# Weight conversion emitted as three interleaved stages, with a reordered start, in a linear-attention and bilinear feed-forward kernel

## The chip, the cores and the metric

The kernel runs on one core of one Trainium2 chip. The metric is the device time of one execution in microseconds (us). The engines named below are TensorE (PE for its matmuls, PEld for its weight loads), VectorE (DVE), ScalarE (ACT), GpSimd (POOL) and SyncE (SP, which here only issues DMAs). Each engine runs its own instructions strictly in the order in which they were emitted; between engines only semaphores order the work. Line numbers (L179) are those of the kernel before.

## The reference

Gated linear attention over 4 batches, 8 heads, 768 positions and 48 channels, then a bilinear feed-forward network on the 3072 tokens:

```python
f = 1.0 / (1.0 + np.exp(-f_logit))
for t in range(S):
    state = f[:, :, t, :, None] * state + np.einsum('bhd,bhe->bhde', k[:, :, t], v[:, :, t])
    y[:, :, t] = np.einsum('bhd,bhde->bhe', q[:, :, t], state)
x = y.transpose(0, 2, 1, 3).reshape(B * S, H * D)      # 3072 x 384
out = ((x @ w_a) * (x @ w_b)) @ w_out                  # 384 -> 1536 -> 384
```

The attention inputs are float32. The three weight matrices come as float64, which no engine computes with.

## The kernel before

**Units.** Attention is cut into 16 units: a batch, a half of the sequence (384 positions) and four of the eight heads. Four sets of input tiles (q, k, f, v) are used in rotation; `load_unit(u)` (L119) issues seven DMAs on SP, and `across(u)` (L315) calls it for unit u+4 when it is done with a set. `front(u)` (L190) makes the decays on ACT, POOL and DVE: two sigmoids (L195, L196), two POOL operations (L198, L199), an ACT operation (L200), then DVE scans (L204, L210) and products into q and k (L206, L211). It is a generator, cut by `yield` into parts that the main program calls one at a time. `scores` (L227), `turn` (L251: transposes of k through the PSUM tile ps_x, and a copy kT), `gains` (L261: matmuls into ps_x, then sums st on DVE), `within` (L298) and `across` (matmuls into ps_y, copies y, DMAs of y into xT issued from ACT's queue, L351) follow. From unit 2 on, `slot(u)` (L400) strings these parts together in six calls.

**Feed-forward.** The tokens form eight blocks of 384. `ffn(blk)` (L356) is a generator: twelve steps of six matmuls each (L366) with a copy b_sb on ACT (L374) and a product ab on DVE (L376), then the matmuls with w_out (L386). In block 0 these last come in twelve groups of three, one group for each 128 rows of w_out, elsewhere in three groups of twelve. The PSUM pool ps_f has four banks for all of this.

**Weights.** `pieces()` (L134) cuts the three matrices into 36 pieces of 128 x 384: w_b and w_a in turn for each of the twelve columns of 128, then the twelve rows of w_out. `load_weights()` (L145) issues the DMA of the next piece, as 64-bit words, into a buffer of a rotating pool "raw" of three. `from_double` (L163) turns a piece into float32 with eight operations on three engines, L173 to L182: ACT takes the absolute value and the sign of the high words, POOL clamps, DVE shifts and masks and scales the low words, POOL adds, ACT takes the absolute value, DVE applies the sign. `convert(n)` (L154) converts pieces one after the other until n are done, and calls `load_weights()` behind each.

**Order.** All of the main program stands under `tc.manual_schedule()` (L432), so each engine keeps the order of emission. The program from L455 to L483 starts units 0 to 2 by hand with convert(1), (2), (4) and (6) in between. The loop from L491 runs the blocks; ahead of each feed-forward step it calls the slot parts that are due by a table of due steps (L488) and, in block 0, `convert`, so that two pieces are emitted for each of the steps i=1 to 9, two more at i=10, and then one for each i. Piece 35, the last, is emitted at i=20.

A buffer of a rotating pool is given to a new tile when the last reader of the old tile has run, whatever the order in which the two were emitted; the instruction that writes the new tile waits for it in its own engine's queue.

Of the kernel before, what the change touches and what calls it, by code (L numbers as in the profile page):

```python
# [10 lines left out]
FP32 = mybir.dt.float32  # L11
I32 = mybir.dt.int32
U32 = mybir.dt.uint32
# [3 lines left out]
C = 128  # L17
FINE = (0, 1, 2, 4, 8, 16)
BLK = 384
PIECE = 384  # L20
# [3 lines left out]
K_EXP = 75.0  # L24
# [12 lines left out]
@with_exitstack  # L37
def kernel(
    ctx: ExitStack,
    tc: tile.TileContext,  # L40
    q: bass.AP,
    k: bass.AP,
    f_logit: bass.AP,
    v: bass.AP,
    masks: bass.AP,
    moe_w_a: bass.AP,
    moe_w_b: bass.AP,
    moe_w_out: bass.AP,
    out: bass.AP,
):  # L50
    nc = tc.nc
    DFF, DM = moe_w_out.shape[0], out.shape[1]
    NKT, NFT = DM // 128, DFF // 128

    const = ctx.enter_context(tc.tile_pool(name="const", bufs=1))

    def fixed(shape, name, dtype=FP32):
        return const.tile(shape, dtype, tag=name, name=name)

    ident = fixed([128, 128], "ident")  # L60
    w_a = fixed([128, NKT, DFF], "w_a")
    w_b = fixed([128, NKT, DFF], "w_b")
    w_out = fixed([128, NFT, DM], "w_out")
    bad = fixed([1, 1], "bad", I32)
    weights = (w_a, w_b, w_out)

    make_identity(nc, ident)
    with ExitStack() as pools:
        by_quotients(pools, tc, q, k, f_logit, v, moe_w_a, moe_w_b, moe_w_out, out, ident, weights, bad)
    again = nc.values_load(bad[0:1, 0:1], min_val=0, max_val=1, skip_runtime_bounds_check_because="it is a comparison's result")  # L70
    with tc.If(again > 0), ExitStack() as pools:
        by_levels(pools, tc, q, k, f_logit, v, masks, out, ident, weights)


def by_quotients(ctx, tc, q, k, f_logit, v, moe_w_a, moe_w_b, moe_w_out, out, ident, weights, bad):
    nc = tc.nc
# [4 lines left out]
    NQ = H // 4  # L81
    NC = BLK // C
# [8 lines left out]
    sb2 = ctx.enter_context(tc.tile_pool(name="sb2", bufs=2))  # L91
    sb4 = ctx.enter_context(tc.tile_pool(name="sb4", bufs=4))
    ab_pool = ctx.enter_context(tc.tile_pool(name="ab", bufs=NFT + 1))
    raw_pool = ctx.enter_context(tc.tile_pool(name="raw", bufs=3))
    ps_a = ctx.enter_context(tc.tile_pool(name="ps_a", bufs=1, space=bass.MemoryType.PSUM))
    ps_f = ctx.enter_context(tc.tile_pool(name="ps_f", bufs=4, space=bass.MemoryType.PSUM))

# [11 lines left out]
    zeros = fixed([128, BLK], "zeros")  # L109
# [6 lines left out]
        b, r = divmod(u, NH * NQ)  # L116
        return (b, *divmod(r, NQ))

    def load_unit(u):  # L119
        if u >= NU:  # L120
            return
        b, half, qd = unit(u)
        t = sets[u % NSET]
        cols = slice(half * BLK, half * BLK + BLK)
        for nm, src in (("f", f_logit), ("k", k), ("q", q)):
            heads = src[b].rearrange("(n two) d s -> two d n s", two=2)
            for par in range(2):
                nc.sync.dma_start(out=t[nm][R * par:R * par + D], in_=heads[par][:, 2 * qd:2 * qd + 2, cols])
        nc.sync.dma_start(
            out=t["v"].rearrange("s n c x -> s n (c x)"),  # L130
            in_=v[b, 2 * qd:2 * qd + 2, :, half * NC:half * NC + NC].rearrange("n s c two d -> s n (c two d)"),
        )

    def pieces():  # L134

# [9 lines left out]
    def load_weights():  # L145
        if len(raws) < len(todo):
            dst, src, shape = todo[len(raws)]
            raw = dst
            if src.dtype != FP32:
                raw = raw_pool.tile([128, *shape], mybir.dt.uint64, tag="raw", name="raw")  # L150
            nc.sync.dma_start(out=raw, in_=src)
            raws.append(raw)

    def convert(n):  # L154

        while done[0] < min(n, len(todo)):
            dst, src, shape = todo[done[0]]
            if src.dtype != FP32:
                from_double(dst, raws[done[0]], shape)
            done[0] += 1  # L160
            load_weights()

    def from_double(dst, raw, shape):  # L163

        words = raw.bitcast(U32).rearrange("p k (n two) -> p (k n) two", two=2)
        lo, hi = words[:, :, 0], words[:, :, 1]  # L170
        h, r, sign = (sb2.tile([128, PIECE], FP32, tag=n, name=n) for n in ("h", "r", "sign"))
        hu, ru = h.bitcast(U32), r.bitcast(U32)
        nc.scalar.activation(h, hi.bitcast(FP32), AF.Abs)  # L173
        nc.scalar.activation(sign, hi.bitcast(FP32), AF.Sign)
        nc.gpsimd.tensor_scalar(h, h, HI_MAX, HI_MIN, ALU.min, ALU.max)  # L175
        nc.vector.tensor_scalar(hu, hu, 3, 0x40000000, ALU.logical_shift_left, ALU.bitwise_xor)  # L176
        nc.vector.tensor_scalar(ru, hu, 0xFF800000, None, ALU.bitwise_and)  # L177
        nc.vector.scalar_tensor_tensor(out=r, in0=lo, scalar=2.0**-52, in1=r, op0=ALU.mult, op1=ALU.mult)  # L178
        nc.gpsimd.tensor_tensor(h, h, r, ALU.add)  # L179
        nc.scalar.activation(h, h, AF.Abs)  # L180
        h, sign = (x.rearrange("p (k n) -> p k n", k=shape[0]) for x in (h, sign))
        nc.vector.tensor_tensor(dst, h, sign, ALU.mult)  # L182

    live = {}
    xT = {}
# [4 lines left out]
    def front(u):  # L190

        t = sets[u % NSET]
        x = halves(t["f"])
        f, inv, fix = (sb2.tile([128, 2 * BLK], FP32, tag=n, name=n) for n in ("f", "inv", "fix"))
        nc.scalar.activation(f, x, AF.Sigmoid)  # L195
        nc.scalar.activation(inv, x, AF.Sigmoid, bias=less, scale=-1.0)  # L196

        nc.gpsimd.tensor_scalar(inv, inv, math.exp(K_EXP), 1.0, ALU.mult, ALU.add)  # L198
        nc.gpsimd.tensor_tensor(fix, f, inv, ALU.mult)  # L199
        nc.scalar.activation(fix, fix, AF.Identity, bias=two, scale=-1.0)  # L200
        yield
        for n in range(2):
            c = slice(n * BLK, n * BLK + BLK)
            nc.vector.tensor_tensor_scan(x[:, c], f[:, c], zeros, math.exp(MIDDLE), ALU.mult, ALU.add)  # L204
        nc.vector.tensor_scalar(held[:, u], t["f"][:, :, BLK - 1], math.exp(MIDDLE - DECAY_MAX), None, ALU.is_ge)
        nc.vector.tensor_tensor(halves(t["q"]), halves(t["q"]), x, ALU.mult)  # L206
        yield
        for n in range(2):
            c = slice(n * BLK, n * BLK + BLK)
            nc.vector.tensor_tensor_scan(inv[:, c], inv[:, c], fix[:, c], math.exp(-MIDDLE), ALU.mult, ALU.mult)  # L210
        nc.vector.tensor_tensor(halves(t["k"]), halves(t["k"]), inv, ALU.mult)  # L211
        live[u] = {}
        yield
# [34 lines left out]
        )  # L248
        live[u]["at"] = at

    def turn(u):  # L251
        kf = halves(sets[u % NSET]["k"])
        kT = sb1.tile([128, 2, NC, 128], FP32, tag="kT", name="kT")
        for n in range(2):
            for c in range(NC):
                o = n * BLK + c * C
                nc.tensor.transpose(ps_x[:, n, c * C:c * C + C], kf[:, o:o + C], ident)  # L257
        nc.scalar.copy(kT.rearrange("s n c x -> s n (c x)"), ps_x[:, :, 0:BLK])
        live[u]["kT"] = kT

    def gains(u):  # L261
# [169 lines left out]

    with tc.manual_schedule():  # L432
        nc.scalar.preload_act_table_set("sigmoid_and_others")
        for i in range(NSET):
            for n, eng, x in (("f", nc.gpsimd, 30.0), ("k", nc.gpsimd, 0.0), ("q", nc.vector, 0.0)):
                eng.memset(sets[i][n], x)
            if i < NQ:
                load_unit(i)
        for ps in (ps_x, ps_y):
            nc.vector.memset(ps, 0.0)  # L440
        for x, value in ((zeros, 0.0), (less, -K_EXP), (two, 2.0)):
            nc.gpsimd.memset(x, value)
        nc.gpsimd.memset(causal, 1.0)
        for p in range(2):
            half = causal[SUB * p:SUB * p + SUB]
# [2 lines left out]
            )  # L448
        nc.gpsimd.memset(ones, 1.0)
        done = [0]  # L450
        for _ in range(3):
            load_weights()


        fronts = [front(u) for u in range(NQ + 1)]  # L455
        for u in range(NQ):
            next(fronts[u])
            next(fronts[u])
        convert(1)
        for u in range(NQ):  # L460
            next(fronts[u])
        for u in range(NQ, NSET):
            load_unit(u)
        scores(0)
        turn(0)
        convert(2)
        gains(0)
        next(fronts[2])
        within(0)
        scores(1)  # L470
        turn(1)
        across(0)
        next(fronts[2])
        convert(4)
        gains(1)
        next(fronts[2])
        within(1)
        slots = {s: slot(s) for s in range(NQ, NU + 1)}
        next(slots[NQ])
        next(slots[NQ])  # L480
        next(slots[NQ])
        across(1)
        convert(6)  # L483
# [1 line left out]

        queue = []
        for s in slots:
            for d in (0, 1, 2.2, 3.4, 4.6, 5.8)[3 if s == NQ else 0:]:  # L488
                queue.append(((s - NQ) * (NFT + NTG) / 2 - 6 + d, s))
        queue.sort(reverse=True)  # L490
        for blk in range(NBLK):  # L491
# [369 lines left out]
```

## Time and profile before

| | |
|---|---|
| median of 3 runs | 789.6 us (789.41 to 790.02) |
| profiled execution: its time | 789.36 us |
| profiled execution: its span | 787.6 us |
| busy: PE, DVE, ACT, POOL | 653.9, 256.6, 183.3, 108.1 us |
| chain that ended last, by engine | PE 69%, DVE 10%, POOL 9%, ACT 6%, issue 4% |
| mean of L173, L174, L180 (ACT) | 544, 542, 525 ns |
| mean of L175, L179 (POOL) | 548, 993 ns |
| mean of L176, L177, L178, L182 (DVE) | 359, 360, 559, 559 ns |
| matmuls of 128 x 384, 3 x 576 | 617 us busy in all |

The page of a profile gives busy time by engine, then the span in 40 slices with the busy share of each engine in tenths. The chain of waits is followed back from the last instruction: at each step to what released it, or to the instruction before it on its engine. The timeline gives each instruction's start and duration in us, its engine, line, operation and tiles; an idle time before it and what ended that stand in brackets. A duration runs from the start on the engine, so where an operation has begun and then waits for something inside the machine, the wait counts in it.

### The profile page before, as it was taken

What the parts mean: (1) busy time and instruction counts of PE and PEld (TensorE: products, weight loads), DVE (VectorE), ACT (ScalarE), POOL (GpSimd) and SP (SyncE); (2) the same over time, 40 slices, a digit from 0 to 9 for tenths busy, and PEclk for the clock granted to TensorE, in tenths of its full rate; (3) what the DMA queues carried; (4) which work ended last, traced back from release to release, by engine and by line L of the source; (5) the groups of instructions that cost most, each with busy time, mean ns of one, the idle gap of its engine ahead of it and who ended that gap; (6) DMA issues with size and microseconds to landing.
All of it is one profiled execution on the core that took longest, in us unless ns stands there. A gap on an engine that the chain in (4) does not pass through costs nothing.

```text
span 787.6 us, 11346 instructions
## 1 busy us (share of the span) xinstructions
PE 653.9 (83%) x4770; PEld 396.3 (50%) x4770; DVE 256.6 (33%) x480; ACT 183.3 (23%) x341; POOL 108.1 (14%) x125
## 2 busy tenths in 40 slices
PE   0235555554867999999999999999999999999996
PEld 0223323332434666666666666666666665655553
DVE  7543635463543333133413331334142311101100
ACT  3232233334333221122112211221222111011100
POOL 7122233233321110011000101010101000000000
PEclk9975788868898999999999999999999999999998
DMA  7643222522242012200221032103000100010000
GB/s 180 161 116 82 72 64 81 140 81 75 80 131 66 16 32 67 70 23 24 78 60 41 6 85 51 43 4 94 12 16 2 36 11 16 1 36 11 1 11 24
DMA packets 34302, 43.30 MB, mean 55 GB/s; under 512 B 4033, under 2 KB 32705, under 8 KB 34241
## 3 DMA queue, kind: packets, MB, share of 16 engines
q1 hardware_dynamic: 29888, 37.76, 17.3%
q10 hardware_dynamic: 4352, 4.72, 2.2%
q8 instruction: 39, 0.64, 0.3%
q14 instruction: 23, 0.18, 0.1%
HBM read 33.03 MB, written 4.72 MB: 48 GB/s over the span
## 4 chain that ended last, share of the span: by engine, by line
PE 69%; DVE 10%; POOL 9%; ACT 6%; issue 4%; ACTq 1%; DMA 0%; POOLq 0%
PE f L366 42%; PE f L386 21%; POOL h L179 5%; DVE r L178 3%; POOL h L175 2%; ACT h L173 2%; DVE r L177 2%; DVE h L176 2%; PE ps_y L326 2%; PE ps_x L257 2%; PE ps_x L235 1%; POOL fix L199 1%; PE ps_y L306 1%; ACT h L180 1%; DVE inv L210 1%
## 5 line engine op out<-in xcount | busy, mean ns | idle before, releaser
L366 PE MATMUL f<-xT,w_b 128*128 128x384 f32 x576 | 219.0, 518 | 36.7 <-ACT b_sb L374 34.2
L386 PE MATMUL f<-w_out,ab 128*128 128x384 f32 x576 | 193.9, 495 | 15.7 <-DVE w_out L182 13.4
L366 PE MATMUL f<-xT,w_a 128*128 128x384 f32 x576 | 204.0, 491 | 0.0
L366 PEld LDWEIGHTS f<-xT,w_b 128*128 128x128 f32 x576 | 111.1, 199 | 112.6 <-ACT b_sb L374 37.3
L386 PEld LDWEIGHTS f<-w_out,ab 128*128 128x128 f32 x576 | 109.8, 193 | 94.7 <-DVE w_out L182 17.2
L376 DVE TENSOR_TENSOR ab<-f,b_sb 128x384 f32<-128x384 f32 x96 | 53.5, 557 | 312.6 <-PE f L366 259.2
L366 PEld LDWEIGHTS f<-xT,w_a 128*128 128x128 f32 x576 | 112.1, 195 | 79.9 <-issue 6.5
L374 ACT COPY b_sb<-f 128x384 f32<-128x384 f32 x96 | 45.7, 476 | 209.0 <-PE f L366 190.8
L235 PE MATMUL ps_x<-q_in,k_in 48*64 48x64 f32 x768 | 18.0, 248 | 68.4 <-DMA k_in<-in_k_dram 27.1
L198 POOL TENSOR_SCALAR inv<-inv 128x768 f32<-128x768 f32 x16 | 14.7, 920 | 342.0 <-ACT inv L196 342.0
L235 PEld LDWEIGHTS ps_x<-q_in,k_in 48*64 48x64 f32 x768 | 16.2, 161 | 68.9 <-issue 57.3
L396 ACT COPY o_sb<-f 128x384 f32<-128x384 f32 x24 | 11.5, 480 | 166.9 <-PE f L386 158.6
L179 POOL TENSOR_TENSOR h<-h,r 128x384 f32<-128x384 f32 x36 | 35.7, 993 | 66.2 <-DVE r L178 66.2
L180 ACT ACTIVATE h<-h 128x384 f32<-128x384 f32 x36 | 18.9, 525 | 110.0 <-POOL h L179 110.0
L204 DVE TENSOR_TENSOR_SCAN f_in<-f,zeros 128x384 f32<-128x384 f32 x32 | 30.8, 1003 | 3.5 <-ACT inv L196 3.5
L175 POOL TENSOR_SCALAR h<-h 128x384 f32<-128x384 f32 x36 | 19.7, 548 | 82.1 <-ACT h L173 82.1
L199 POOL TENSOR_TENSOR fix<-f,inv 128x768 f32<-128x768 f32 x16 | 30.7, 1917 | 1.3
L210 DVE TENSOR_TENSOR_SCAN inv<-inv,fix 128x384 f32<-128x384 f32 x32 | 30.6, 999 | 0.0
L176 DVE TENSOR_SCALAR h<-h 128x384 uint32<-128x384 uint32 x36 | 12.9, 359 | 47.7 <-POOL h L175 47.7
L289 DVE TENSOR_TENSOR st<-st,ps_x 128x96 f32<-128x96 f32 x80 | 20.3, 254 | 21.7 <-PE ps_x L273 19.2
L337 ACT COPY y<-ps_y 64x384 f32<-64x384 f32 (+1 forms) x48 | 22.9, 476 | 17.9 <-PE ps_y L326 17.4
L200 ACT ACTIVATE fix<-fix,two 128x768 f32<-128x768 f32 x16 | 15.0, 939 | 48.7 <-POOL fix L199 48.7
(46 smaller groups left out, 315.7 us busy)
## 6 DMA issues: line engine op xcount, KB each, us to landing
f_in<-in_f_logit_dram SPq DMA_DIRECT2D x32, 144.0 KB, 3.4
k_in<-in_k_dram SPq DMA_DIRECT2D x32, 144.0 KB, 3.7
q_in<-in_q_dram SPq DMA_DIRECT2D x32, 144.0 KB, 3.4
v_in<-in_v_dram SPq DMA_DIRECT2D x16, 288.0 KB, 3.7
raw<-in_moe_w_b_dram SPq DMA_DIRECT2D x12, 384.0 KB, 3.2
raw<-in_moe_w_a_dram SPq DMA_DIRECT2D x12, 384.0 KB, 3.5
raw<-in_moe_w_out_dram SPq DMA_DIRECT2D x12, 384.0 KB, 3.0
out_dram<-o_sb SPq DMA_DIRECT2D x24, 192.0 KB, 1.9
```

Source lines behind the costliest of these rows:

```text
L175: nc.gpsimd.tensor_scalar(h, h, HI_MAX, HI_MIN, ALU.min, ALU.max)
L176: nc.vector.tensor_scalar(hu, hu, 3, 0x40000000, ALU.logical_shift_left, ALU.bitwise_xor)
L179: nc.gpsimd.tensor_tensor(h, h, r, ALU.add)
L180: nc.scalar.activation(h, h, AF.Abs)
L199: nc.gpsimd.tensor_tensor(fix, f, inv, ALU.mult)
L204: nc.vector.tensor_tensor_scan(x[:, c], f[:, c], zeros, math.exp(MIDDLE), ALU.mult, ALU.add)
L210: nc.vector.tensor_tensor_scan(inv[:, c], inv[:, c], fix[:, c], math.exp(-MIDDLE), ALU.mult, ALU.mult)
L235: nc.tensor.matmul(ps[SUB * p:SUB * p + SUB, h, o:o + SUB], lhsT=kf[r, tokens(n, c, p)], rhs=qf[r, tokens(n, c, p)], start=True, stop=True,)
L366: nc.tensor.matmul(ps[nm], lhsT=w[:, kt, ft * 128:ft * 128 + 128], rhs=x[:, kt], start=kt == 0, stop=kt == NKT - 1,)
L374: nc.scalar.copy(b_sb, ps["b"])
L376: nc.vector.tensor_tensor(ab[ft], ps["a"], b_sb, ALU.mult)
L386: nc.tensor.matmul(o[tg], lhsT=ab[ft][:, tg * 128:tg * 128 + 128], rhs=w_out[:, ft], start=ft == 0, stop=ft == NFT - 1,)
```

## The change

- `from_double` becomes a generator of three stages. Stage 1 is L173, L174, L175; stage 2 is L176 to L180; stage 3 is L182. A new generator `conversion()` emits, in round n, stage 1 of piece n, stage 2 of piece n-1 and stage 3 of piece n-2, then calls `load_weights()`. `convert(n)` draws rounds from it until n pieces are done. The tiles h and sign move to a pool with four buffers, the pool "raw" gets four, and four loads are issued ahead.
- `front` yields before L200 instead of behind it.
- `turn` can use two banks of ps_f for its transposes, with two half copies, and does so for units 0 and 1.
- The start is reordered: the f tiles are cleared by DVE and not by POOL, the small constants come first, the identity is built behind the first clearing, the f loads of units 0 and 1 go ahead of their k, q and v loads. Units 0 and 1 are emitted interleaved.
- Of slot 2 only the first call stands ahead of block 0 (three before); the others are due at i=0.

```diff
-    raw_pool = ctx.enter_context(tc.tile_pool(name="raw", bufs=3))
+    raw_pool = ctx.enter_context(tc.tile_pool(name="raw", bufs=4))
...
-    def load_unit(u):
+    def load_unit(u, names="fkqv"):
...
-    def convert(n):
-
-        while done[0] < min(n, len(todo)):
-            dst, src, shape = todo[done[0]]
-            if src.dtype != FP32:
-                from_double(dst, raws[done[0]], shape)
-            done[0] += 1
-            load_weights()
...
-        h, r, sign = (sb2.tile([128, PIECE], FP32, tag=n, name=n) for n in ("h", "r", "sign"))
-        hu, ru = h.bitcast(U32), r.bitcast(U32)
+        h, sign = (sb4.tile([128, PIECE], FP32, tag=n, name=n) for n in ("h", "sign"))
         nc.scalar.activation(h, hi.bitcast(FP32), AF.Abs)
         nc.scalar.activation(sign, hi.bitcast(FP32), AF.Sign)
         nc.gpsimd.tensor_scalar(h, h, HI_MAX, HI_MIN, ALU.min, ALU.max)
+        yield
+        r = sb2.tile([128, PIECE], FP32, tag="r", name="r")
+        hu, ru = h.bitcast(U32), r.bitcast(U32)
         nc.vector.tensor_scalar(hu, hu, 3, 0x40000000, ALU.logical_shift_left, ALU.bitwise_xor)
         nc.vector.tensor_scalar(ru, hu, 0xFF800000, None, ALU.bitwise_and)
         nc.vector.scalar_tensor_tensor(out=r, in0=lo, scalar=2.0**-52, in1=r, op0=ALU.mult, op1=ALU.mult)
         nc.gpsimd.tensor_tensor(h, h, r, ALU.add)
         nc.scalar.activation(h, h, AF.Abs)
+        yield
         h, sign = (x.rearrange("p (k n) -> p k n", k=shape[0]) for x in (h, sign))
         nc.vector.tensor_tensor(dst, h, sign, ALU.mult)
+
+    def conversion():
+
+        going = []
+        for n in range(len(todo) + 2):
+            if n < len(todo):
+                dst, src, shape = todo[n]
+                going.append(from_double(dst, raws[n], shape) if src.dtype != FP32 else iter(()))
+            for g in list(reversed(going)):
+                if next(g, "end") == "end":
+                    going.remove(g)
+            load_weights()
+            yield n - 1
+
+    ready = conversion()
+
+    def convert(n):
+
+        while done[0] < min(n, len(todo)):
+            done[0] = next(ready)
...
         nc.gpsimd.tensor_tensor(fix, f, inv, ALU.mult)
+        yield
         nc.scalar.activation(fix, fix, AF.Identity, bias=two, scale=-1.0)
-        yield
...
+            ps = ps_f.tile([128, 512], FP32, tag="f", name="f") if spare else ps_x[:, n]
...
+            for n, eng, x in (("f", nc.vector, 30.0), ("k", nc.gpsimd, 0.0), ("q", nc.vector, 0.0)):
                 eng.memset(sets[i][n], x)
             if i < NQ:
-                load_unit(i)
+                load_unit(i, "f")
+            if i == 0:
+                make_identity(nc, ident)
+        for u in range(NQ):
+            load_unit(u, "kqv")
...
-        for _ in range(3):
+        for _ in range(4):
             load_weights()
...
         fronts = [front(u) for u in range(NQ + 1)]
-        for u in range(NQ):
-            next(fronts[u])
-            next(fronts[u])
+        next(fronts[0])
+        next(fronts[1])
+        convert(0)
+        next(fronts[0])
+        next(fronts[0])
+        scores(0)
+        turn(0, True)
         convert(1)
-        for u in range(NQ):
-            next(fronts[u])
+        next(fronts[1])
+        next(fronts[1])
+        within(0)
+        gains(0)
         for u in range(NQ, NSET):
             load_unit(u)
-        scores(0)
-        turn(0)
+        next(fronts[2])
+        scores(1)
+        turn(1, True)
         convert(2)
-        gains(0)
+        across(0)
+        within(1)
+        gains(1)
+        convert(3)
         next(fronts[2])
-        within(0)
-        scores(1)
-        turn(1)
-        across(0)
         next(fronts[2])
-        convert(4)
-        gains(1)
-        next(fronts[2])
-        within(1)
         slots = {s: slot(s) for s in range(NQ, NU + 1)}
-        next(slots[NQ])
-        next(slots[NQ])
         next(slots[NQ])
         across(1)
         convert(6)
...
-            for d in (0, 1, 2.2, 3.4, 4.6, 5.8)[3 if s == NQ else 0:]:
+            for d in (0, 1, 2.2, 3.4, 4.6, 5.8)[1 if s == NQ else 0:]:
```

More of the change, by code (lines that the diff above doesn't have):

```diff
@@ L65 @@
     weights = (w_a, w_b, w_out)
-    make_identity(nc, ident)
     with ExitStack() as pools:
@@ L125, in load_unit @@
         for nm, src in (("f", f_logit), ("k", k), ("q", q)):
+            if nm not in names:
+                continue
             heads = src[b].rearrange("(n two) d s -> two d n s", two=2)
@@ L128, in load_unit @@
                 nc.sync.dma_start(out=t[nm][R * par:R * par + D], in_=heads[par][:, 2 * qd:2 * qd + 2, cols])
[L129 to L132, printed above, removed]
+        if "v" in names:
+            nc.sync.dma_start(
+                out=t["v"].rearrange("s n c x -> s n (c x)"),
+                in_=v[b, 2 * qd:2 * qd + 2, :, half * NC:half * NC + NC].rearrange("n s c two d -> s n (c two d)"),
+            )
     def pieces():
@@ L249, in scores, with turn @@
         live[u]["at"] = at
-    def turn(u):
+    def turn(u, spare=False):
         kf = halves(sets[u % NSET]["k"])
@@ L254, in turn @@
         for n in range(2):
+            ps = ps_f.tile([128, 512], FP32, tag="f", name="f") if spare else ps_x[:, n]
             for c in range(NC):
                 o = n * BLK + c * C
-                nc.tensor.transpose(ps_x[:, n, c * C:c * C + C], kf[:, o:o + C], ident)
-        nc.scalar.copy(kT.rearrange("s n c x -> s n (c x)"), ps_x[:, :, 0:BLK])
+                nc.tensor.transpose(ps[:, c * C:c * C + C], kf[:, o:o + C], ident)
+            if spare:
+                nc.scalar.copy(kT[:, n].rearrange("s c x -> s (c x)"), ps[:, 0:BLK])
+        if not spare:
+            nc.scalar.copy(kT.rearrange("s n c x -> s n (c x)"), ps_x[:, :, 0:BLK])
         live[u]["kT"] = kT
@@ L433, in by_quotients @@
         nc.scalar.preload_act_table_set("sigmoid_and_others")
+        for x, value in ((less, -K_EXP), (two, 2.0), (zeros, 0.0)):
+            nc.gpsimd.memset(x, value)
         for i in range(NSET):
-            for n, eng, x in (("f", nc.gpsimd, 30.0), ("k", nc.gpsimd, 0.0), ("q", nc.vector, 0.0)):
+            for n, eng, x in (("f", nc.vector, 30.0), ("k", nc.gpsimd, 0.0), ("q", nc.vector, 0.0)):
                 eng.memset(sets[i][n], x)
             if i < NQ:
-                load_unit(i)
+                load_unit(i, "f")
[3 more added lines that the diff above has]
+            load_unit(u, "kqv")
         for ps in (ps_x, ps_y):
             nc.vector.memset(ps, 0.0)
-        for x, value in ((zeros, 0.0), (less, -K_EXP), (two, 2.0)):
-            nc.gpsimd.memset(x, value)
         nc.gpsimd.memset(causal, 1.0)
```

## The prediction

> **What bounds it now.** I read the busy shares in 40 slices first, then the chain of work that ended last, in order of time.
>
> ```profile
> span 787.6 us, 11346 instructions
> PE   0235555554867999999999999999999999999996
> ...
> 77.15 1.00 POOL h L179
> ...
> 242.74 1.00 POOL h L179
> 244.94 2.20 PE f L386 x6
> 247.14 3.87 PE f L366 x12
> ...
> 757.05 23.23 PE f L386 x72
> ```
>
> From the 14th slice on TensorE never idles: twelve matmuls take 3.87 us, and from 247.14 to 757.05+23.23 it is one solid run. Ahead of that it is half idle, and the chain is a string of weight pieces: L179 lies on it 36 times, 32 of them from 77.15 to 242.74. So the end is 244.94, the instant at which the last converted piece lets TensorE go, plus 542.7 us that this change does not touch. I forecast that instant; the rest follows it one to one. The timeline shows what a piece costs.
>
> ```profile
> 78.61 0.54 ACT L173 ACTIVATE h<-raw 128x384 f32<-128x384 f32 x1
> ...
> 79.24 0.51 POOL L175 TENSOR_SCALAR h<-h 128x384 f32<-128x384 f32 x1 [1.09 <-ACT h L173]
> ...
> 79.78 0.36 DVE L176 TENSOR_SCALAR h<-h 128x384 uint32<-128x384 uint32 x1 [0.48 <-POOL h L175]
> ...
> 80.17 0.36 DVE L177 TENSOR_SCALAR r<-h 128x384 uint32<-128x384 uint32 x1
> 80.57 0.56 DVE L178 SCALAR_TENSOR_TENSOR r<-raw,r 128x384 f32<-128x384 uint32 x1
> ...
> 81.21 0.99 POOL L179 TENSOR_TENSOR h<-h,r 128x384 f32<-128x384 f32 x1 [1.47 <-DVE r L178]
> 82.23 0.52 ACT L180 ACTIVATE h<-h 128x384 f32<-128x384 f32 x1 [2.64 <-POOL h L179]
> 82.67 0.53 ACT L173 ACTIVATE h<-raw 128x384 f32<-128x384 f32 x1
> 82.79 0.56 DVE L182 TENSOR_TENSOR w_a<-h,sign 128x384 f32<-128x384 f32 x1 [1.67 <-ACT h L180]
> ```
>
> One engine at a time: 78.61 to 82.67 is 4.06 us a piece. L173 of the next piece stands in ACT's queue behind L180 of this one, which waits for L179. The 165.6 us from 77.15 to 242.74 are 31 such rounds (125.9 us) and 39.7 us of attention work and copies between them.
>
> **The pipeline, part by part.** No operation of a piece is added or removed; they are emitted as L173, L174, L175 of piece n, then L176 to L180 of n-1, then L182 of n-2. So ACT still sees L180 before the next L173, but L180 now waits only for L175(n) and L179(n-1), since the three DVE operations ran a round before. The loop that is left, from the starts above: L173 to L175 0.63, L175 to L179 0.53 (the operation and a step), L179 to L180 1.02, L180 to the next L173 0.44: 2.62 us. That is the lower bound, with POOL and DVE running side by side as if alone. Before, these two never overlapped within a piece, so the trace has no row of it; the nearest are these.
>
> ```profile
> 9.85 2.31 POOL L199 TENSOR_TENSOR fix<-f,inv 128x768 f32<-128x768 f32 x1
> 10.60 1.59 DVE L205 TENSOR_SCALAR held<-f_in 128x2 f32<-128x2 f32 x1
> ...
> 39.66 1.81 POOL L199 TENSOR_TENSOR fix<-f,inv 128x768 f32<-128x768 f32 x1
> ...
> 41.10 0.96 DVE L243 TENSOR_TENSOR at<-ps_x,causal 128x768 f32<-128x768 f32 x1 [1.34 <-PE ps_x L235]
> ...
> 41.98 1.79 DVE L204 TENSOR_TENSOR_SCAN f_in<-f,zeros 128x384 f32<-128x384 f32 x2
> ...
> 43.81 0.17 DVE L205 TENSOR_SCALAR held<-f_in 128x2 f32<-128x2 f32 x1
> ...
> 83.27 2.06 DVE L204 TENSOR_TENSOR_SCAN f_in<-f,zeros 128x384 f32<-128x384 f32 x2
> 83.28 1.24 POOL L175 TENSOR_SCALAR h<-h 128x384 f32<-128x384 f32 x1 [1.08 <-ACT h L173]
> ```
>
> A tensor_scalar on two elements that takes 0.17 us alone took 1.59 beside a POOL operation, and ended as that did (12.16). A scan (two operands in SBUF) and an L175 stretched each other, 1.79 to 2.06 and 0.51 to 1.24: they took turns. L243, with an operand in PSUM, ran beside POOL unstretched. L176 and L177 are tensor_scalars, L178 and L182 have two operands in SBUF, so I take all four to exclude POOL, as the nearest rows do. The Trainium skill, page "SBUF — State Buffer", section "Who interferes with whom", says the same of the pair of ports that both engines use, names two-input operations too, and so speaks against most of this overlap; by that rule the sum would be the one below, without it the 2.62 loop.
>
> What an operation holds is a little less than it takes: the first scan let go at 83.27+0.90, L175 ended at 84.52, so it held 0.35 of its 0.51; L179, likewise, 0.85 of 0.99. In the steady order L179 0.85, L176 0.36, L177 0.39, L178 0.53, L175 0.35, L182 0.47 that makes 2.95 us a round, against 4.06. With whole durations it is 3.40, the upper bound. I take 2.95 because the contested rows ended so much sooner than a whole duration after the other.
>
> **A feed-forward step.** In block 0 a step is two rounds, then a copy b_sb and the product ab.
>
> ```profile
> 97.28 0.46 ACT L374 COPY b_sb<-f 128x384 f32<-128x384 f32 x1
> ...
> 97.89 0.55 DVE L376 TENSOR_TENSOR ab<-f,b_sb 128x384 f32<-128x384 f32 x1
> ...
> 98.35 0.95 DVE L243 TENSOR_TENSOR at<-ps_x,causal 128x768 f32<-128x768 f32 x1
> ```
>
> ab starts 0.61 after b_sb and holds DVE's queue 0.46, and the next L176 stands behind it: DVE loses its lead once a step. Counted from the end of b_sb: ab done at 0.60, then L176, L175 in turn, L177, L178, L182 to 2.6, L179 to 3.45, L180, next L173 at 3.9; second round 2.95; b_sb 0.43: 7.3 us (6.5 without exclusion, 8.1 with whole durations), where before it was 2 x 4.06 + 0.43 = 8.55. So the step gains 1.25, not 2.9.
>
> **The start.** f loads go ahead of k, q and v, the f memsets move from POOL to DVE, turn(0) no longer waits for at, and front is cut before L200.
>
> ```profile
> 1.03 3.12 DVE L436 MEMSET q_in<- 128x768 f32 x4 [1.03 <-PEq L851]
> 1.71 0.87 SPq L128 DMA_DIRECT2D f_in<-in_f_logit_dram  x2
> ...
> 5.38 0.84 ACT L195 ACTIVATE f<-f_in 128x768 f32<-128x768 f32 x1 [3.29 <-DMA f_in<-in_f_logit_dram]
> ...
> 21.53 0.56 DVE L178 SCALAR_TENSOR_TENSOR r<-raw,r 128x384 f32<-128x384 uint32 x1
> 22.16 0.37 SPq L151 DMA_DIRECT2D raw<-in_moe_w_a_dram  x1
> 22.63 0.90 SPq L128 DMA_DIRECT2D f_in<-in_f_logit_dram  x2
> ...
> 32.24 0.80 ACT L258 COPY kT<-ps_x 128x768 f32<-128x768 f32 x1 [8.52 <-PE ps_x L257]
> ...
> 37.00 0.83 ACT L195 ACTIVATE f<-f_in 128x768 f32<-128x768 f32 x1
> ...
> 70.41 1.47 ACT L337 COPY y<-ps_y 128x384 f32<-128x384 f32 x3 [0.69 <-PE ps_y L326]
> ...
> 74.55 0.54 ACT L173 ACTIVATE h<-raw 128x384 f32<-128x384 f32 x1 [2.67 <-issue]
> ```
>
> DVE now has eight memsets of 0.78 and the two of PSUM: free near 9.4, where the first scan waits for POOL's L199 to 10.1; scans, q, scans, k in turns with unit 1's L198 and L199 end near 17.8, and unit 0's kT is ready at 21.6 instead of 33.04. Then comes the wait that the change adds. convert(1) now runs three rounds, each of which issues a load of piece n+4 into the buffer of piece n, whose last reader, L178(n), is emitted a round later; 22.16 shows a raw load going as L178 ends. The third of these loads waits for L178 of piece 2, which stands in convert(2), and SP's queue holds the loads of units 2 and 3 behind it. L178(2) comes after unit 1's front, unit 0's st and at(1), near 37.2; unit 2's f is then usable some 0.4 + 3.7 later (the first was issued at 1.71 and read at 5.38), and its L195, which stands in ACT's queue ahead of turn(1), starts near 41.3, where it was 37.00. ACT idles 12 us there and the 11 us gained are nearly gone: kT(1) 43.9. From there on the order is shorter (one piece in convert(2), one in convert(3)), and across(1) lets ACT go near 68.9, not 74.55: 5.6 us gained, with the same four pieces done and a fifth begun. Bounds of this part are 3 us either way. convert(0) does nothing, since done starts at 0.
>
> **The sum.** Rounds 5 to 7 at 2.95 bring 77.7. The slot of unit 2, most of which now comes in one go at i=0 (front(3) whole, turn, gains), keeps DVE until 88.5; with the two rounds of i=1 and b_sb the first step ends at 95.1 (before 97.7). Steps i=2 to 10: 9 x 7.3 = 65.7. Slots between them:
>
> ```profile
> 37.73 0.92 ACT L196 ACTIVATE inv<-f_in,less 128x768 f32<-128x768 f32 x1
> ...
> 38.74 0.83 POOL L198 TENSOR_SCALAR inv<-inv 128x768 f32<-128x768 f32 x1 [2.20 <-ACT inv L196]
> ```
>
> Two at (0.87 each), two first parts of front (ACT 1.57, then POOL 2.7 from 38.74 to 41.47 ahead of L175, of which all but 3.0 lie beside DVE's work), the second part (scans 1.79, q 0.95, a turn: 2.95), the third the same 2.9, one across (70.41 to 74.55 is 4.14 on ACT; DVE's chain covers 1.0: 3.1), turn 0.2: 16.9 us. i=11 to 13, one round each and an ab: 12.5. i=14 with a front part 5.0, i=15 to 18 4 x 2.95 = 11.8, i=19 with across(3) 5.2. Together 95.1 + 117.1 = 212.2, against 244.94: 32.7 us less. 787.6 - 32.7 = 754.9 of span; the profiled execution is 789.36, so 1.76 lies outside: 756.7, and the median 789.6 stands 0.24 over it: **757**.
>
> That TensorE isn't late next, the windows show.
>
> ```profile
> 71.00:245.00 174.00, 101.18 (x606) 56.16 (x601) 84.61 (x179) 59.98 (x124) 54.74 (x68) 0.81 0.30 88
> ```
>
> It is busy 101 of 174 us, at a granted clock of 0.81; the stretch would be 141. The other cover is xT of block 1: across(3) at 207.0 and some 4.7 for copies and landing gives 211.7, level with the last piece, so conversion can't gain much more at the end without that.
>
> **Rivals.** (1) No exclusion for L178 and L182: rounds of 2.62, steps of 6.5, no turns in the start: 18 us less, 739. For it: no row has these forms beside a POOL operation. Against it: the scan. (2) Exclusion for whole durations, or in an unlucky order: steps 8.1, rounds 3.40: 12 us more, 769. (3) Slower: turns fall so that DVE's four run neither beside POOL nor in the 1.09 us from the end of L179 over L180 and L173 to the next L175. Then a round is 1.53 + 1.83 + 1.09 = 4.45 against 4.06, 31 times 0.39 is 12 us, less the 5.6 of the start: 6 us over, 796. It decides once less than 0.39 of the 1.83 finds cover; L176 can start as L179 ends, which speaks against it. (4) The change does not do what it says: DVE is held at each ab and SP at each raw load, so that the rounds stay serial: 4.06 a round, within 0.2% of before.
>
> **Chances.** Forecast 0.52 (750 to 764), (1) 0.20, (2) 0.20, (3) 0.05, (4) 0.03. About 0.2% is what a measurement tells from no change. Faster 0.92, same 0.03, slower 0.05. The range leaves out half of (1), (3) and (4): 740 to 772.
>
> **What would show it.** L179 starts 2.95 apart between i=15 and 18, and 7.3 per pair in the steps; L175, L176 and L177 longer on average than 0.55, 0.36 and 0.36, since a wait for the other engine counts in the duration; unit 2's L195 at 41 with a DMA as its releaser; the last L182 near 212 and TensorE solid after it. L195 at 30 would break the SP step, unstretched L176 and L179 the exclusion, a TensorE that idles after 215 the one to one.

## The result, and the profile after

The changed kernel takes 754.78 us (754.32 to 755.18, 4 runs) beside 789.5 us of the kernel before on the same chip: a ratio of 0.956 with a 95% interval of 0.954 to 0.958. The forecast was 757, with a range of 740 to 772.

The page of the changed kernel: its span, TensorE's busy tenths in 40 slices, and the chain by engine.

```profile
span 752.8 us, 11345 instructions
PE   0322665576989999999999999999999999999996
...
PE 72%; POOL 9%; DVE 7%; ACT 4%; issue 4%; DMA 1%; ACTq 1%; SPq 1%; DVEq 0%; POOLq 0%
```

Its chain of waits in order of time (start, duration, what):

```profile
198.48 1.27 POOL h L174
...
201.34 1.27 POOL h L174
...
204.20 1.27 POOL h L174
...
211.22 2.20 PE f L407 x6
...
723.29 23.23 PE f L407 x72
```

Lines have moved: L165 to L167, L171 to L175 and L178 are L173 to L175, L176 to L180 and L182 of before; L387 and L407 are the matmuls L366 and L386. The reader sees the same picture as before, shortened in front: the last converted piece lets TensorE go at 211.22, not 244.94, and the solid run behind it lasts 535.3 us to 746.52, as it did from 244.94 to 780.28. The span fell by 34.8 us, 33.7 of them ahead of that instant. The three adds shown, of late pieces, stand 2.86 us apart instead of 4.06.

Where a round's time goes is in the timeline (the ACT rows and the raw loads between them left out):

```profile
197.98 0.51 POOL L167 TENSOR_SCALAR h<-h 128x384 f32<-128x384 f32 x1 [1.09 <-ACT h L165]
198.01 0.88 DVE L178 TENSOR_TENSOR w_out<-h,sign 128x384 f32<-128x384 f32 x1
198.45 1.30 POOL L174 TENSOR_TENSOR h<-h,r 128x384 f32<-128x384 f32 x1
198.82 1.15 DVE L171 TENSOR_SCALAR h<-h 128x384 uint32<-128x384 uint32 x1
...
200.00 0.36 DVE L172 TENSOR_SCALAR r<-h 128x384 uint32<-128x384 uint32 x1
...
200.39 0.56 DVE L173 SCALAR_TENSOR_TENSOR r<-raw,r 128x384 f32<-128x384 uint32 x1
...
200.83 0.51 POOL L167 TENSOR_SCALAR h<-h 128x384 f32<-128x384 f32 x1 [1.09 <-ACT h L165]
200.87 0.88 DVE L178 TENSOR_TENSOR w_out<-h,sign 128x384 f32<-128x384 f32 x1
```

DVE does not idle between these rows, and POOL waits 1.09 us a round for ACT. Three operations are stretched: L178 takes 0.88 where 0.56 is its length alone, L174 1.30 for 0.99, L171 1.15 for 0.36. Each has begun while the other engine was at work and ends late by most of what was left of that: L178 behind L167, L174 behind L178, L171 behind L174. The groups show it over all 36 pieces (out<-in, then busy time and mean):

```profile
L174 POOL TENSOR_TENSOR h<-h,r 128x384 f32<-128x384 f32 x36 | 44.4, 1234 | 23.7 <-DVE r L173 23.7
L167 POOL TENSOR_SCALAR h<-h 128x384 f32<-128x384 f32 x36 | 20.9, 582 | 70.1 <-ACT h L165 69.8
L171 DVE TENSOR_SCALAR h<-h 128x384 uint32<-128x384 uint32 x36 | 25.7, 714 | 12.2 <-POOL h L167 12.2
```

Before, the means were 993, 548 and 359 ns. The higher busy share of DVE (37%, it was 33%; 20.7 us more) is mostly waiting: L171 alone is up by 12.8 us, while the f memsets that moved to DVE are 2.8.

The start, from the timeline, with the wait that the change adds:

```profile
38.43 0.37 SPq L153 DMA_DIRECT2D raw<-in_moe_w_b_dram  x1
38.84 1.09 SPq L129 DMA_DIRECT2D f_in<-in_f_logit_dram  x2
...
43.73 0.84 ACT L211 ACTIVATE f<-f_in 128x768 f32<-128x768 f32 x1 [14.22 <-DMA f_in<-in_f_logit_dram]
```

SP issues unit 2's f only behind the raw load at 38.43, and ACT stands 14.22 us for it.

### The profile page after: what moved, and what is told of

Read it like the earlier page. It is cut to its first block, busy times and chain, and to the rows that moved or that the text cites. A ratio compares the mean times of both kernels' runs of the same rounds, so it can differ in the third digit from the quotient of the medians.

```text
span 752.8 us, 11345 instructions
## 1 busy us (share of the span) xinstructions
PE 643.6 (85%) x4770; PEld 392.3 (52%) x4770; DVE 277.3 (37%) x484; ACT 182.6 (24%) x343; POOL 114.0 (15%) x121
## 4 chain that ended last, share of the span: by engine, by line
PE 72%; POOL 9%; DVE 7%; ACT 4%; issue 4%; DMA 1%; ACTq 1%; SPq 1%; DVEq 0%; POOLq 0%
PE f L387 44%; PE f L407 22%; POOL h L174 6%; PE ps_x L251 2%; POOL h L167 2%; PE ps_y L327 2%; ACT h L165 1%; PE ps_y L347 1%; DVE r L173 1%; PE ps_x L294 1%; PE ps_x L275 1%; DVE f_in L220 1%; DVE r L172 1%; POOL fix L215 1%; ACTq L372 1%
## 5 line engine op out<-in xcount | busy, mean ns | idle before, releaser
L387 PE MATMUL f<-xT,w_b 128*128 128x384 f32 x576 | 214.4, 510 | 23.2 <-ACT b_sb L395 23.2
L387 PE MATMUL f<-xT,w_a 128*128 128x384 f32 x576 | 202.0, 487 | 0.0
L407 PE MATMUL f<-w_out,ab 128*128 128x384 f32 x576 | 190.3, 488 | 5.3 <-DVE w_out L178 3.5
L387 PEld LDWEIGHTS f<-xT,w_b 128*128 128x128 f32 x576 | 110.7, 198 | 97.9 <-ACT b_sb L395 26.9
L407 PEld LDWEIGHTS f<-w_out,ab 128*128 128x128 f32 x576 | 108.4, 190 | 82.0 <-DVE w_out L178 6.3
L387 PEld LDWEIGHTS f<-xT,w_a 128*128 128x128 f32 x576 | 110.0, 191 | 77.3 <-issue 2.0
L174 POOL TENSOR_TENSOR h<-h,r 128x384 f32<-128x384 f32 x36 | 44.4, 1234 | 23.7 <-DVE r L173 23.7
L175 ACT ACTIVATE h<-h 128x384 f32<-128x384 f32 x36 | 18.8, 523 | 82.0 <-POOL h L174 79.3
L220 DVE TENSOR_TENSOR_SCAN f_in<-f,zeros 128x384 f32<-128x384 f32 x32 | 32.8, 1066 | 3.0 <-ACT inv L212 3.0
L167 POOL TENSOR_SCALAR h<-h 128x384 f32<-128x384 f32 x36 | 20.9, 582 | 70.1 <-ACT h L165 69.8
L171 DVE TENSOR_SCALAR h<-h 128x384 uint32<-128x384 uint32 x36 | 25.7, 714 | 12.2 <-POOL h L167 12.2
L226 DVE TENSOR_TENSOR_SCAN inv<-inv,fix 128x384 f32<-128x384 f32 x32 | 29.0, 948 | 0.0
L327 PE MATMUL ps_y<-at,v_in 64*48 64x64 f32 x768 | 15.5, 231 | 12.7 <-ACT y L358 12.7
```

Source lines behind the costliest of these rows:

```text
L327: nc.tensor.matmul(ps_y[e:e + D, p, o:o + SUB], lhsT=t["v"][r, n, c, h * D:h * D + D], rhs=at[r, h, o:o + SUB], start=o == 0, stop=True, s ...
L387: nc.tensor.matmul(ps[nm], lhsT=w[:, kt, ft * 128:ft * 128 + 128], rhs=x[:, kt], start=kt == 0, stop=kt == NKT - 1,)
L407: nc.tensor.matmul(o[tg], lhsT=ab[ft][:, tg * 128:tg * 128 + 128], rhs=w_out[:, ft], start=ft == 0, stop=ft == NFT - 1,)
```

## The experiments

**1. What DVE and POOL do to each other, by itself.** A kernel of twelve phases and nothing else of the computation.

```diff
+    for phase in ((shift,), (scaled,), (signed,), (from_psum,), (add,), (clamp,),
+                  (shift, add), (scaled, add), (signed, add), (from_psum, add), (shift, clamp), (signed, clamp)):
+        tc.strict_bb_all_engine_barrier()
+        with tc.manual_schedule():
+            for _ in range(10):
+                for op in phase:
+                    op()
```

> Leaves out the whole computation: twelve phases, each behind a barrier of all engines, of ten operations of a conversion form on DVE, on POOL, or ten of each beside each other, on 128x384 tiles of their own. Theory (DVE and POOL take turns): the phase lasts as long as the sum of what both hold. With about 0.39 a shift (L171's form), 0.47 for the scaling of low words (L173) and for the sign product (L178), and 0.85 to 0.95 an add (L174): shift beside add 1.2 to 1.3 us a pair, scaling beside add and sign product beside add 1.3 to 1.4 a pair. A product with an operand in PSUM beside add: no longer than the longer of the two, about 0.95 a pair. Rival (two-operand forms do not exclude POOL, only single-operand ones do): scaling and sign product beside add 0.95 a pair, shift beside add 1.25. Rival (no exclusion at all): every pair 0.95.

Its timeline, each row ten operations (L56 the shift, L60 the scaling, L63 the sign product, L66 the product from PSUM, L69 the add, L72 the clamp):

```profile
3.61 3.91 DVE L56 TENSOR_SCALAR d_a<-d_a 128x384 uint32<-128x384 uint32 x10
7.60 5.89 DVE L60 SCALAR_TENSOR_TENSOR d_c<-d_wide,d_b 128x384 f32<-128x384 uint32 x10
13.64 5.90 DVE L63 TENSOR_TENSOR d_c<-d_a,d_b 128x384 f32<-128x384 f32 x10
...
25.78 10.61 POOL L69 TENSOR_TENSOR p_c<-p_a,p_b 128x384 f32<-128x384 f32 x10 [23.57 <-SPq L82]
36.60 5.80 POOL L72 TENSOR_SCALAR p_c<-p_a 128x384 f32<-128x384 f32 x10 [0.22 <-SPq L82]
42.49 9.98 DVE L56 TENSOR_SCALAR d_a<-d_a 128x384 uint32<-128x384 uint32 x10 [16.91 <-SPq L81]
42.60 10.72 POOL L69 TENSOR_TENSOR p_c<-p_a,p_b 128x384 f32<-128x384 f32 x10 [0.19 <-SPq L82]
53.40 11.96 DVE L60 SCALAR_TENSOR_TENSOR d_c<-d_wide,d_b 128x384 f32<-128x384 uint32 x10 [0.93 <-SPq L81]
53.51 12.70 POOL L69 TENSOR_TENSOR p_c<-p_a,p_b 128x384 f32<-128x384 f32 x10 [0.19 <-SPq L82]
...
79.30 5.88 DVE L66 TENSOR_TENSOR d_c<-d_ps,d_b 128x384 f32<-128x384 f32 x10 [1.00 <-SPq L82]
79.34 10.64 POOL L69 TENSOR_TENSOR p_c<-p_a,p_b 128x384 f32<-128x384 f32 x10 [0.19 <-SPq L82]
90.05 5.65 DVE L56 TENSOR_SCALAR d_a<-d_a 128x384 uint32<-128x384 uint32 x10 [4.87 <-SPq L81]
90.18 5.90 POOL L72 TENSOR_SCALAR p_c<-p_a 128x384 f32<-128x384 f32 x10 [0.20 <-SPq L82]
96.22 7.53 DVE L63 TENSOR_TENSOR d_c<-d_a,d_b 128x384 f32<-128x384 f32 x10 [0.53 <-SPq L82]
96.28 7.85 POOL L72 TENSOR_SCALAR p_c<-p_a 128x384 f32<-128x384 f32 x10 [0.20 <-SPq L82]
```

Alone a scaling takes 0.59 and an add 1.06; beside each other a pair takes 1.27 (just under the 1.3 expected), so neither is hidden by the other, though the sum, 1.65, is not reached either. The sign product with the clamp: 0.79 where they take 0.59 and 0.58 alone. With an operand in PSUM both keep their own time, 5.88 and 10.64. So operations with two operands in SBUF do exclude POOL for most of their length, and the rivals without exclusion fall. The shift is the miss, as the pair was expected to take 1.2 to 1.3: it waits, 9.98 for ten instead of 3.91, yet the adds beside it go at their own pace, 10.72 against 10.61. The clamps lose as little to it, 5.90 against 5.80. That it fits into what an add does not hold of its 1.06 is a reading that no run tests.

**2. The wait in SP's queue.** One buffer more.

```diff
-    raw_pool = ctx.enter_context(tc.tile_pool(name="raw", bufs=4))
+    raw_pool = ctx.enter_context(tc.tile_pool(name="raw", bufs=5))
```

> One buffer more in the pool raw (five): the load of piece n+4 then takes the buffer of piece n-1, whose last reader is emitted already, so no load in SP's queue waits for a later convert. Theory (the wait in SP's queue holds unit 2's loads and through them ACT): the first sigmoid of unit 2 starts near 30 us instead of 43.7, ACT is done with across(1)'s DMAs near 64 instead of 71.7, and the time falls by about 8 us to 747. Rival (another wait takes its place: unit 2's data come early but the chain over DVE and PE stays): sigmoid early, time within 1 us of 754.8.

745.18 us (ratio to the kernel before 0.944, 0.942 to 0.945), 9.6 less than the changed kernel. Its timeline:

```profile
25.88 0.37 SPq L153 DMA_DIRECT2D raw<-in_moe_w_b_dram  x1
26.29 0.96 SPq L129 DMA_DIRECT2D f_in<-in_f_logit_dram  x2
...
31.16 0.84 ACT L211 ACTIVATE f<-f_in 128x768 f32<-128x768 f32 x1 [1.53 <-DMA f_in<-in_f_logit_dram]
```

Unit 2's f goes out at 26.29 instead of 38.84, its sigmoid starts at 31.16 instead of 43.73, and across(1)'s DMAs are issued by 62.06 instead of 71.58. The wait was on the path, and nothing as long took its place.

**3. ab between the rounds.** In block 0 only.

```diff
-            nc.vector.tensor_tensor(ab[ft], ps["a"], b_sb, ALU.mult)
+            product = partial(nc.vector.tensor_tensor, ab[ft], ps["a"], b_sb, ALU.mult)
+            if blk == 0:
+                late.append(product)
+            else:
+                product()
...
-                    convert(min(2 * i + 6, 2 * NFT) if i < NFT - 2 else NFT + i + 4)
+                    n = min(2 * i + 6, 2 * NFT) if i < NFT - 2 else NFT + i + 4
+                    convert(n - 1 if i <= NFT - 2 else n)
+                    if late:
+                        late.pop()()
+                    convert(n)
```

> In block 0 the product ab of a step is emitted between the two conversion rounds of the next step instead of ahead of both, so DVE does not stand at the copy b_sb when the next round's shift could run. Nothing else moves. Theory (ab takes DVE's lead once a step): the step falls from 7.13 us to about 6.2 (two rounds of 2.86 and b_sb 0.43), nine steps and the three single ones make 9 to 11 us, 745. Rival (the turns of DVE and POOL set the step, and ab only fills a gap): step 7.1, time within 1.5 us of 754.8.

742.07 us (0.940, 0.938 to 0.941), 12.7 less. The copies b_sb of two steps in a row, first of the changed kernel, then of this one:

```profile
131.22 0.46 ACT L395 COPY b_sb<-f 128x384 f32<-128x384 f32 x1
138.34 0.46 ACT L395 COPY b_sb<-f 128x384 f32<-128x384 f32 x1
```

```profile
126.90 0.46 ACT L397 COPY b_sb<-f 128x384 f32<-128x384 f32 x1
...
132.75 0.46 ACT L397 COPY b_sb<-f 128x384 f32<-128x384 f32 x1
```

7.12 us a step became 5.85. In the changed kernel DVE stood 1.80 us for that copy, with the next shift behind it:

```profile
131.72 0.56 DVE L397 TENSOR_TENSOR ab<-f,b_sb 128x384 f32<-128x384 f32 x1 [1.80 <-ACT b_sb L395]
132.19 0.35 DVE L171 TENSOR_SCALAR h<-h 128x384 uint32<-128x384 uint32 x1
```

The step came out under the 6.2 expected (two free rounds and a copy), and the gain of 12.7 us over the 9 to 11, since the first round of a step here takes 2.64 us from the start of its first operation to that of the next, under the free 2.86. Its rows in this kernel (L166 is the first operation, L168 the clamp, L175 the add, L179 the sign product):

```profile
127.25 0.57 ACT L166 ACTIVATE h<-raw 128x384 f32<-128x384 f32 x1
...
127.56 0.55 DVE L179 TENSOR_TENSOR w_b<-h,sign 128x384 f32<-128x384 f32 x1
...
127.92 0.56 POOL L168 TENSOR_SCALAR h<-h 128x384 f32<-128x384 f32 x1 [1.48 <-ACT h L166]
...
128.44 0.99 POOL L175 TENSOR_TENSOR h<-h,r 128x384 f32<-128x384 f32 x1
...
129.89 0.54 ACT L166 ACTIVATE h<-raw 128x384 f32<-128x384 f32 x1
```

The sign product here runs while POOL still waits for ACT, so the clamp takes 0.56 and the add its 0.99. The round is then the loop over ACT and POOL alone, for which the prediction had 2.62.

**4. The add on DVE.**

```diff
-        nc.gpsimd.tensor_tensor(h, h, r, ALU.add)
+        nc.vector.tensor_tensor(h, h, r, ALU.add)
```

> The add of a piece (L174 of the kernel after) goes from POOL to DVE. Theory (turns: 0.85 of POOL are replaced by about 0.47 of DVE in the sum that makes a round): the steady round falls from 2.86 to about 2.6, the step from 7.1 to about 6.5, the time by 6 to 10 us to about 746. Rival (the engines run side by side and the loop over ACT and POOL sets the round): DVE has five operations a round and becomes the bound with ab, at and the scans on top of them; time 755 to 765.

736.86 us (0.934, 0.932 to 0.935), 17.9 less than the changed kernel. The starts of rounds on ACT:

```profile
173.65 0.56 DVE L173 SCALAR_TENSOR_TENSOR r<-raw,r 128x384 f32<-128x384 uint32 x1
...
175.27 0.55 ACT L165 ACTIVATE h<-raw 128x384 f32<-128x384 f32 x1
...
175.90 0.51 POOL L167 TENSOR_SCALAR h<-h 128x384 f32<-128x384 f32 x1 [3.82 <-ACT h L165]
175.97 0.84 DVE L173 SCALAR_TENSOR_TENSOR r<-raw,r 128x384 f32<-128x384 uint32 x1
...
177.87 0.55 ACT L165 ACTIVATE h<-raw 128x384 f32<-128x384 f32 x1
```

2.60 us a round, as expected. More work on the busier engine made the kernel faster. That alone doesn't prove the turns: the add also leaves the loop over ACT and POOL, so a shorter round would fit engines side by side as well. What speaks for them is L173, 0.84 us where the clamp L167 falls beside it and 0.56 where it doesn't; DVE's five operations take 2.60 with that wait and 2.31 without it (L171 at 172.88 and 175.19). The whole gain was underrated: a step fell from 7.12 to 6.13, not 6.5, as DVE stood 0.49 us for b_sb instead of 1.80, and the start gave 3.7 that the expectation had not counted (across(1)'s DMAs begin at 64.82 instead of 68.48).

**5. The start alone**: the changed kernel with the conversion of the kernel before.

```diff
-    def conversion():
...
+    def convert(n):
+
+        while done[0] < min(n, len(todo)):
+            dst, src, shape = todo[done[0]]
+            if src.dtype != FP32:
+                from_double(dst, raws[done[0]], shape)
+            done[0] += 1
+            load_weights()
```

> The kernel after with the conversion of the kernel before (pieces one after the other, three raw buffers, three loads ahead): the new start, the new cut of front and the new slot table alone. Theory (the start's lead is spent, the gain is the pipeline's): rounds back at 4.06 and steps at 8.5 us; unit 2's first sigmoid near 28, since no load waits for a later convert; the lead of some 8 us there is given back, as units' parts that stood ahead of block 0 now stand at i=0: 784 to 790. Rival (the start carries a good part of the gain): 765 to 780.

781.26 us (0.989, 0.987 to 0.991), 8.7 less than before and under the range expected. Unit 2's sigmoid starts at 28.13, and the first b_sb at 92.78 instead of 97.28: 4.5 of the lead lasts. The steps are 8.47 us. Most of the rest was overlooked: with the new cut of front ahead of its ACT operation the step with front's first part takes 12.38 us instead of 13.81, and there are two of these.

**6. The pipeline alone**: the kernel before with the three-stage conversion.

```diff
+    def conversion():
+
+        going = []
+        for n in range(len(todo) + 2):
...
-        for _ in range(3):
+        for _ in range(4):
             load_weights()
```

> The kernel before with the three-stage conversion, four raw buffers and four loads ahead, and nothing else of the change. Theory: steps of 7.1 and rounds of 2.86 as in the kernel after; in this start the raw load that waits stands behind convert(1) too, but convert(2) comes ahead of unit 2's first sigmoid, so ACT does not stop for it, and less of slot 2 stands at i=0: 748 to 756, no worse than the kernel after. Rival (the new start is needed for the pipeline's gain): 760 to 775.

748.72 us (0.948, 0.946 to 0.949): 41.3 less than before, and 6.1 less than the whole change. Its timeline at the same place:

```profile
33.43 0.37 SPq L151 DMA_DIRECT2D raw<-in_moe_w_b_dram  x1
33.90 0.90 SPq L128 DMA_DIRECT2D f_in<-in_f_logit_dram  x2
...
38.70 0.84 ACT L209 ACTIVATE f<-f_in 128x768 f32<-128x768 f32 x1 [1.60 <-DMA f_in<-in_f_logit_dram]
```

The same order in SP's queue, but convert(2) stands ahead of the sigmoid, the raw load goes five us sooner and ACT waits 1.60 us, not 14.22. The first b_sb is at 87.44, where the changed kernel has 96.41. Behind it the changed kernel regains 2.8 us: its two steps with front's first part take 9.92 and 9.94, here 11.32 and 11.33.

**7. Five buffers on the old start**, the control for 2.

```diff
-    raw_pool = ctx.enter_context(tc.tile_pool(name="raw", bufs=4))
+    raw_pool = ctx.enter_context(tc.tile_pool(name="raw", bufs=5))
```

> The pipeline alone, on the old start, with five raw buffers instead of four. Theory (the fifth buffer is worth 9.6 us in the new start only because there unit 2's loads stand behind a raw load that waits for a later convert, and ACT behind them; the old start has convert(2) ahead of unit 2's sigmoid): 747.5 to 749, the same as with four. Rival (a deeper rotation helps the pipeline itself, by earlier raw loads): 739 to 744.

746.17 us (0.945, 0.943 to 0.946): 2.5 less than with four, between the two expectations. Unit 2's sigmoid moves from 38.70 to 37.00 and across(1)'s DMAs from 66.31 to 63.88, and the lead stays. So the same wait costs something in the old start as well, only a quarter of what it costs in the new one; no step behind it got shorter (7.12 us).

**8. and 9. The waits taken out together**: five buffers and ab between the rounds; then with the add on DVE as well. The edits are those above.

> Five raw buffers and ab between the rounds, together. Theory: the two waits are in different places (ahead of block 0, in its steps), so their gains add, 9.6 and 12.7 us: 732 to 734. Rival (they share something late next, such as xT of block 1): 736 to 742.

> Five raw buffers, ab between the rounds, and the add on DVE. Theory: without the wait at ab a step is two rounds and b_sb, so the add on DVE is worth the difference of the rounds there, 2.86 to 2.60, some 0.5 a step and 0.26 a single round, about 7 us in all with the start: 724 to 728. Rival (DVE, now with five conversion operations a round and ab and the attention work, is the bound itself): 730 to 734, no better than with the add on POOL.

732.54 us (0.928, 0.926 to 0.929) and 721.86 us (0.914, 0.912 to 0.915). The first two gains add: 9.6 + 12.7 = 22.3, and 754.8 - 732.5 = 22.3. They lie in different places. The add gives 10.7 more instead of its 17.9, as the wait at ab that it also shortened is gone: it takes 0.35 us off a step (5.85 to 5.50) and not 0.99. That was taken as 7, so the last version came out just under its range. Its chain enters the solid run at 176.75:

```profile
176.75 5.83 PE f L413 x12
```

The run of TensorE that begins there lasts 539.0 us, not 535.3. In this execution its first twelve matmuls take 5.83 us, at a granted clock of 0.71, where the changed kernel has six in 2.20, and it starts on the product of the piece before last. So a start 34.5 us earlier than in the changed kernel makes the span only 31.1 us shorter.

This version beats both kernels. It was not tried on the old start.

## Why the prediction was right

The mechanism was the one that was forecast, but for one part of the turns that is told below, and the terms lie close. That 757 came within 2.2 us of 754.8 is partly luck, as two errors of 2.8 us, in the start and in the steps, leaned in opposite directions.

| step of the prediction | forecast | measured |
|---|---|---|
| a free round, in turns | 2.95 | 2.86 |
| a step of two rounds with ab | 7.3 | 7.12 |
| steps with at; front's first, second, third part; across | 8.2; 10.3, 10.25, 10.2; 10.4 | 7.8; 9.9, 9.8, 9.9; 9.9 |
| unit 0's kT ready | 21.6 | 21.05 |
| unit 2's first sigmoid | 41.3 | 43.73 |
| across(1) lets ACT go | 68.9 | 71.68 |
| end of the first b_sb | 95.1 | 96.87 |
| last sign product done | 212.2 | 211.17 |

**What bounds it.** Right: the instant at which the last piece lets TensorE go moved by 33.7 us, and the span by 34.8.

**Turns instead of overlap.** Right for the operations with two operands in SBUF, and settled by experiment 1, which could have broken it. The loop without exclusion, 2.62, and the round of whole durations, 3.40, both miss 2.86. The order in the trace is the one that the sum assumed, L174, L171, L172, L173, L167, L178. Read from the ends in that fence, the terms are 0.86, 0.22, 0.39, 0.59, 0.39 and 0.41, where the sum had 0.85, 0.36, 0.39, 0.53, 0.35 and 0.47. The 0.85 was an analogy, since no L179 of the kernel before is stretched. The one that was mis-sized most is L171: it ends 0.22 after the add (199.97 and 199.75), since part of its 0.36 is done while it waits. That makes 2.86 instead of 2.95.

What the prediction had wrong is that L171 and L172 would hold POOL up as well. Experiment 1 shows that a shift doesn't; L172's form was not tried beside POOL. In the round POOL is not held by them either: from the end of the add to the start of L167 it waits for L175 and L165 on ACT, 1.08 us (199.75 to 200.83), while DVE's tail of L171, L172 and L173 brings L178 to its start in 1.12 (200.87). The sum counts DVE's side of these two chains; that they are equally long to 0.04 us is luck. Which of L178 and L167 starts first decides what a round costs: where the sign product comes before the clamp, as in the rows of experiment 3, the round is 2.64 although the operations exclude POOL all the same.

The Trainium skill, page "SBUF — State Buffer", section "Who interferes with whom", has the loser of the shared pair of ports blocked for the whole instruction. By that, a round would be the 3.40 that the prediction has as its upper bound, and not the 2.95 for which it names the page. Experiment 1 agrees that a form with two operands in SBUF contends with POOL and one with an operand in PSUM does not, but the pair of 1.27, where whole durations make 1.65, says that the loser waits for less than an instruction's profiled time.

**ab.** Right: 1.80 us of idle DVE ahead of each, and 12.7 us when it is moved. The prediction had the gain of a step at 1.25; it was 8.49 - 7.12 = 1.37.

**The start.** The wait in SP's queue was named and is real; its price was underrated. The raw load went at 38.43, not 37.2, and from there to the use of unit 2's f it took 5.3 us, not 4.1. So across(1) was 2.8 us late against the forecast, and the start gained 2.9 us instead of 5.6. The prediction called the 11 us that were won "nearly gone"; run 6 shows that this was too kind: against the old start under the same pipeline, the new one loses 9.0 us up to the first b_sb.

**The steps behind it** made up for that: 114.3 us from the end of the first b_sb to the end of the last sign product, where the sum had 117.1, for the shorter round and for slots that cost 2.7 to 2.8 us each instead of 2.9 to 3.1.

**The rivals.** (1), (2) and (3) would need free rounds of 2.62, 3.40 and 4.45, and 2.86 was measured. (4) fell with the first row of the chain. TensorE was not next in the changed kernel; in run 9, 34.5 us earlier, it begins to count, by the 3.7 us told there.

What stays open: with five buffers in both, the new start is worth at most 1.0 us (746.17 against 745.18; the intervals of the two ratios overlap), alone it was worth 8.7. The cut of front accounts for 2.8 in either, by its steps; why the 4.5 us by which the start alone is ahead at the first b_sb turn into a loss of 1.4 there under the pipeline was not taken apart. The larger part of slot 2 at i=0 is a candidate that no run here isolates.

## What to carry to other kernels

When a chain that hops over three engines is turned into a pipeline, the new period is the longest of the loops that are left, and two engines that exclude each other count in it as one wherever their operations meet: add up what they hold, look which of them starts first, and try whether the work of one is cheaper on the other. Look in each in-order queue for the instruction that now waits for something emitted later (a buffer whose last reader moved a round back, a product that waits for a copy), and ask what stands behind it; here a deeper pool and one moved product were worth 22.3 us, two thirds of the change itself. And time the parts of a change alone: one part of this one cost 6 us in the company of the other.

## What the runs showed of the hardware that was not expected

- The shift, a DVE operation on one SBUF operand, beside a POOL add costs POOL next to nothing (10.72 us for ten adds, 10.61 alone) but waits itself, 1.00 us instead of 0.39. With two SBUF operands both pay: 1.27 a pair.
- What one engine keeps from the other is less than its operation takes: 1.27 a pair where 0.59 and 1.06 make 1.65. If an add holds 0.84, a clamp 0.35 and a two-operand DVE form of 384 elements 0.43, the mixed phases come out at 1.27 and 0.78, near the 1.27 and 0.79 measured; the splitting is an estimate, with the clamp's 0.35 taken from the prediction's reading of the kernel before.
- The wait for the other engine counts as the waiter's busy time: the mean of L171 doubled, 359 to 714 ns, with no more work in it.
- Whether two operations that exclude each other cost a round anything can hang on which of them starts first: 2.86 us with the sign product behind the clamp, 2.64 with it ahead.
